# Banded attention and two FFN layers: four output buffers per tile instead of two

## The chip, the cores and the metric

The kernel runs on one core of one Trainium2 chip. The metric is device time in microseconds, from the start to the end of one execution. The core has five engines that run side by side, each with a queue of its own that it works off in order: TensorE (PE, with its weight loads listed apart as PEld), VectorE (DVE), ScalarE (ACT), GpSimd (POOL) and SyncE (SP), which here only issues DMAs. TensorE writes its results to PSUM, eight banks of 128 x 512 floats; VectorE and ScalarE copy them from there to SBUF, and a DMA takes them from SBUF to device memory.

## What is computed

Attention over a band with sinks, for 4 batches, 8 heads, 768 positions and 64 dimensions a head, and behind it two feed-forward layers over 3072 tokens (512 wide, 2048 hidden), all in float32:

```python
keep = is_sink | in_window                      # first 4 keys, and the last 128
scores = np.where(keep, scale * q @ k.T, -1e9)
a = np.exp(scores - scores.max(-1, keepdims=True))
a = a / (a.sum(-1, keepdims=True) + 1e-9)
x = a @ v                                       # -> 3072 tokens x 512
h = x @ w1_in;  x = (h - np.tanh(h)) @ w1_out   # layer 1
h = np.maximum(x @ w2_in, 0.0)
out = (h * h) @ w2_out                          # layer 2
```

## The kernel before

Float32 products are made from two parts of each operand, a high one and the rest (`split`, lines 147 to 151), with three matmuls for each product: high by high, high by low, low by high. Weights, activations and attention probabilities all go through this.

**Layer 1** (`ffn`, lines 434 to 524) takes the tokens in 8 tiles of 384. A tile walks over 16 chunks of the hidden dimension. `mm1` (12 matmuls, line 451) makes a chunk's hidden values in a PSUM bank, `ps_h`, of which there is one; `act` (lines 455 to 468) forms `h - tanh(h)` in a tile `t` (two buffers) and splits it into `gs`; `mm2` (12 matmuls, lines 483 and 485) adds the chunk's part to the tile's four results, `acc`, one PSUM bank each, four banks in all. A chunk's `mm2` is issued one chunk late, two chunks late in the last tile (`lag`). The tile's last `mm2` therefore runs while the next tile's first chunk is in work, and it ends with the four evictions, lines 487 to 498. Between the matmuls of tile j a hook (`hook`, lines 826 to 843) sets the attention of tile j + 1, head by head, and the conversion of layer 2's weights, piece by piece.

**Layer 2** (`Second`, lines 557 to 788) takes the tokens in 6 tiles of 512, and a tile in 8 groups of 256 hidden units. It makes the first product by seven products of sums of blocks (`first`, `rest`) and the second one directly (`second`), one group late, again with four results in the four `acc` banks, evicted in lines 749 to 757. A tile's inputs come from device memory by four DMAs (`load_x`) into the tiles `xs`; GpSimd makes four sums of them, three in new tiles and one in place (`sum_x`), and ScalarE and GpSimd split seven operands out of them (`split_x`) into `xop`. `xs` has seven buffers, just what a tile's inputs and sums take. The second layer's output weights are fetched group by group into four buffers, named `wi`, `wo`, `wos2` and `wos3` (`fetch_out`, line 609).

**What sets the order.** TensorE's order is that of the source, written out by hand. The instructions of the other engines and of SyncE are put in order at compile time by a planner that steps through the program with estimated times: an instruction is placed once its inputs are there and a buffer for its output is free, and those with the lower number go first. The evictions have their number lowered by 200 (`high_priority`), the DMAs behind them don't. Tiles of one `tag` share its `bufs` buffers: one is handed on to a later tile when all readers of the old tile are done, and the instructions that fill it wait for those readers on the chip. So an eviction into `o` waits, with two buffers, for the store of the result two before it.

Result m of a tile goes to VectorE where m is odd and to ScalarE where it is even. In layer 1 each is copied to `o` (lines 488 to 494) and stored to `x2` in device memory (line 496, `x<-o` in the trace); in layer 2 it is copied to `o` (lines 750 to 756) and stored to the output (line 757, `out_dram<-o`). The branch `l == 1` of `ffn` belongs to `general`, the path for other sinks and windows, which these inputs don't take.

Of the kernel before, what the change touches and what calls it, by code (L numbers as in the profile page):

```python
# [11 lines left out]
F32 = mybir.dt.float32  # L12
# [7 lines left out]
P = 128  # L20
# [4 lines left out]
T = 384  # L25
# [12 lines left out]
HT = T2 // 2  # L38
NG = FC // 2
NP = 7  # L40
# [106 lines left out]
def split(c, dst, src, lo_eng):  # L147

    nc = c.nc
    nc.scalar.activation(dst[:, 0, :], src, AF.Copy)  # L150
    lo_eng.tensor_tensor(dst[:, 1, :], src, dst[:, 0, :].bitcast(F32), ALU.subtract)  # L151
# [282 lines left out]
def ffn(c, layers, xs, hook=None):  # L434


    nc = c.nc
    accs = {}

    def lag(l, j):  # L440
        return 2 if l == 1 or j == NT - 1 else 1

    def mm1(l, j, fc, x, q):
        w = layers[l].get(0, fc).rearrange("p a (k f) -> p a k f", f=P)
        if q == 0:
            tag = ("ps_h", "ps_s", "ps_t", "ps_v")[fc % 4] if l == 1 or j == NT - 1 else "ps_h"
            c.hb = c.ps.tile([P, 512], F32, tag=tag, name=tag, bufs=1)
        h = c.hb
        for kc in range(2 * q, 2 * q + 2):
            for i, (a, b) in enumerate(((0, 0), (0, 1), (1, 0))):  # L450
                nc.tensor.matmul(h[:, :T], w[:, a, kc, :], x[kc][:, b, :], start=(kc == 0 and i == 0),  # L451
                                 stop=(kc == KC - 1 and i == 2))
        return h

    def act(l, h, j, fc):
        t = c.fp.tile([P, T], F32, tag="t", name="t", bufs=2)
        if lag(l, j) > 1 and fc % 2:
            gs = c.spare(fc)[:, : 2 * T].rearrange("p (a t) -> p a t", t=T)
        else:
            gs = c.fp.tile([P, 2, T], F32R, tag="gs", name="gs", bufs=2)  # L460
        if l == 0:
            c.last_a = nc.scalar.activation(t, h[:, :T], AF.Tanh)  # L462
            c.last_d = nc.vector.tensor_tensor(t, h[:, :T], t, ALU.subtract)  # L463
        else:
            c.last_a = nc.scalar.activation(t, h[:, :T], AF.Relu)
            c.last_d = nc.vector.scalar_tensor_tensor(t, h[:, :T], 0.0, t, ALU.max, ALU.mult)
        split(c, gs, t, nc.vector if l > 0 or j > 0 else nc.gpsimd)
        return gs

    def mm2(l, j, fc, gs, q):  # L470
        w = layers[l].get(1, fc)
        if fc == 0 and q == 0:
            accs[l, j] = [c.ps.tile([P, 512], F32, tag="acc", name="acc", bufs=4) for _ in range(KC if l == 0 else T // P)]
        acc = accs[l, j]
        pas = ((0, 0), (0, 1), (1, 0))
        n = len(acc)
        work = [(m, i) for m in range(n) for i in range(3)]
        hw = (len(work) + 1) // 2
        for m, i in work[q * hw : (q + 1) * hw]:
            a, b = pas[i]  # L480
            st = dict(start=(fc == 0 and i == 0), stop=(fc == FC - 1 and i == 2))
            if l == 0:
                nc.tensor.matmul(acc[m][:, :T], w[:, a, ts(m, P)], gs[:, b, :], **st)  # L483
            else:
                nc.tensor.matmul(acc[m], gs[:, b, ts(m, P)], w[:, a, :], **st)
        if fc == FC - 1 and q == 1:
            for m in range(n):
                o = c.fp.tile([P, 512], F32, tag="o", name="o", bufs=2)
                wd = T if l == 0 else 512
                with c.tc.high_priority(offset=200):  # L490
                    if m % 2:
                        nc.vector.tensor_copy(o[:, :wd], acc[m][:, :wd])
                    else:
                        nc.scalar.activation(o[:, :wd], acc[m][:, :wd], AF.Copy)  # L494
                if l == 0:
                    nc.sync.dma_start(c.x2[m, :, ts(j, T)], o[:, :T])
                else:
                    nc.sync.dma_start(c.out[j * T + m * P : j * T + (m + 1) * P, :], o)

    pend = []  # L500
    for l in range(len(layers)):
        for j in range(NT):
            x = xs(l, j)
            for fc in range(FC):
                late = pend[: len(pend) - lag(l, j) + 1]
                pend = pend[len(late) :]
                if hook:
                    hook(l, j, fc, 0)
                mm1(l, j, fc, x, 0)
                if hook:  # L510
                    hook(l, j, fc, 1)
                h = mm1(l, j, fc, x, 1)
                gs = act(l, h, j, fc)
                if hook:
                    hook(l, j, fc, 2)
                for p in late:
                    mm2(*p, 0)
                    if p is late[-1] and hook:
                        hook(l, j, fc, 3)
                    mm2(*p, 1)  # L520
                if not late and hook:
                    hook(l, j, fc, 3)
                pend.append((l, j, fc, gs))
    return [lambda p=p, q=q: mm2(*p, q) for p in pend for q in range(2)]


# [30 lines left out]
class Second:  # L557
# [179 lines left out]
    def second(self, j, g, s, q):  # L737

        c, nc = self.c, self.c.nc
        if g == 0 and q == 0:  # L740
            self.acc = [c.ps.tile([P, 512], F32, tag="acc", name="acc", bufs=4) for _ in range(4)]
        seen = ((1, 1), (0, 0)), ((1, 0), (0, 1))
        for th, f in seen[q]:
            w, gs = self.wo[2 * g + f], s.g[th, f]
            for m in range(2):
                for i, (a, b) in enumerate(((0, 0), (0, 1), (1, 0))):
                    nc.tensor.matmul(self.acc[2 * th + m], gs[:, b, ts(m, P)], w[:, a, :],  # L747
                                     start=(g == 0 and q == 0 and i == 0), stop=(g == NG - 1 and q == 1 and i == 2))
                if g == NG - 1 and q == 1:
                    o = c.fp.tile([P, 512], F32, tag="o", name="o", bufs=2)  # L750
                    k = 2 * th + m
                    with c.tc.high_priority(offset=200):
                        if m:
                            nc.vector.tensor_copy(o, self.acc[k])  # L754
                        else:
                            nc.scalar.activation(o, self.acc[k], AF.Copy)
                    nc.sync.dma_start(c.out[j * T2 + k * P : j * T2 + (k + 1) * P, :], o)
# [222 lines left out]
```

## Time and profile before

| | |
|---|---|
| median of 3 runs | 1304.63 us (1301.48 to 1305.8) |
| the profiled execution | 1303.22 us |
| its span, first to last instruction | 1301.3 us |
| TensorE busy | 1245.7 us, 96% |
| VectorE busy | 816.4 us, 63% |
| ScalarE busy | 644.6 us, 50% |
| GpSimd busy | 396.5 us, 30% |
| DMA | 158.27 MB, mean 122 GB/s |
[...]

The span has four parts: about 54 us with the loads and the attention of the first tile, layer 1 with the attention of the tiles to come until about 790 us, layer 2 until 1294 us, and the last stores. The rows below are given by engine and line. "x6" is a count of instructions, the number in front of the engine is the start in microseconds and the one behind it the time, and square brackets hold the time for which the engine stood idle before the row and what released it. `x<-o` is the DMA from the tile `o` to the buffer `x2`; the program's names stand without numbers.

### The profile page before, as it was taken

What the parts mean: (1) busy time and instruction counts of PE and PEld (TensorE: products, weight loads), DVE (VectorE), ACT (ScalarE), POOL (GpSimd) and SP (SyncE); (2) the same over time, 40 slices, a digit from 0 to 9 for tenths busy, and PEclk for the clock granted to TensorE, in tenths of its full rate; (3) what the DMA queues carried; (4) which work ended last, traced back from release to release, by engine and by line L of the source; (5) the groups of instructions that cost most, each with busy time, mean ns of one, the idle gap of its engine ahead of it and who ended that gap; (6) DMA issues with size and microseconds to landing.
All of it is one profiled execution on the core that took longest, in us unless ns stands there. A gap on an engine that the chain in (4) does not pass through costs nothing.

```text
span 1301.3 us, 21253 instructions
## 1 busy us (share of the span) xinstructions
PE 1245.7 (96%) x7632; PEld 1167.3 (90%) x7632; DVE 816.4 (63%) x2004; ACT 644.6 (50%) x1690; POOL 396.5 (30%) x381
## 2 busy tenths in 40 slices
PE   7888899999899999999999999999999999999997
PEld 5777799999799999999999998999989999999996
DVE  7888667777776677676675675454464544644543
ACT  7766566666566667666665552232232322323221
POOL 1555632323233334343332402050140410503100
PEclk9999899999999999999999999999999999999999
DMA  9641134443333333333322233343352433533432
GB/s 365 245 173 49 54 116 128 127 146 117 95 117 107 119 103 102 114 101 114 116 69 90 89 91 128 105 139 134 109 162 100 130 130 98 162 97 99 140 105 82
DMA packets 67795, 158.27 MB, mean 122 GB/s; under 512 B 6864, under 2 KB 29392, under 8 KB 67680
## 3 DMA queue, kind: packets, MB, share of 16 engines
q1 hardware_dynamic: 67680, 156.82, 37.1%
q8 instruction: 62, 1.02, 0.3%
q14 instruction: 53, 0.43, 0.1%
HBM read 131.63 MB, written 25.17 MB: 120 GB/s over the span
## 4 chain that ended last, share of the span: by engine, by line
PE 72%; DVE 10%; DMA 8%; ACT 4%; issue 2%; POOL 1%; SPq 0%; ACTq 0%; DVEq 0%; POOLq 0%
PE acc L747 20%; PE acc L483 14%; PE ps_h L451 12%; PE ps_h L696 5%; PE ps_v L696 5%; PE ps_t L696 5%; DMA wos<-in_w_in_dram 5%; DVE w_bit L135 3%; PE ps_s L696 3%; DMA x<-o 2%; DVE w_bit L134 2%; PE ps_t L318 2%; DVE w_bit L133 2%; PE ps_s L269 1%; PE ps_v L359 1%
## 5 line engine op out<-in xcount | busy, mean ns | idle before, releaser
L483 PE MATMUL acc<-gs,wo 128*128 128x384 f32 x1440 | 300.4, 346 | 10.3 <-ACT o L494 10.3
L451 PE MATMUL ps_h<-x,wi 128*128 128x384 f32 x1392 | 293.1, 346 | 1.0 <-DVE t L463 1.0
L483 PEld LDWEIGHTS acc<-gs,wo 128*128 128x128 f32 x1440 | 247.9, 190 | 14.3 <-ACT o L494 11.8
L451 PEld LDWEIGHTS ps_h<-x,wi 128*128 128x128 f32 x1392 | 238.1, 189 | 3.8 <-DVE t L463 3.0
L150 ACT ACTIVATE x<-gs 128x256 fp32r<-128x256 f32 x144 | 54.8, 412 | 203.9 <-DVE gs L713 130.1
L151 POOL TENSOR_TENSOR x<-gs,x 128x256 fp32r<-128x256 f32 x48 | 35.6, 741 | 351.0 <-ACT x L150 351.0
L747 PE MATMUL acc<-wos,x 128*128 128x512 f32 x576 | 139.5, 391 | 0.0
L747 PEld LDWEIGHTS acc<-wos,x 128*128 128x128 f32 x576 | 105.2, 188 | 19.9
L463 DVE TENSOR_TENSOR t<-ps_h,t 128x384 f32<-128x384 f32 x116 | 64.7, 557 | 86.9 <-ACT t L462 86.9
L218 POOL TENSOR_TENSOR k_l<-qkv,k_h 128x416 fp32r<-128x416 f32 (+1 forms) x48 | 60.6, 1262 | 113.7 <-ACT k_h L217 113.1
L278 ACT ACTIVATE p<-p,nm 128x272 f32<-128x272 f32 (+1 forms) x168 | 83.5, 497 | 20.7 <-DVE nm L271 19.4
L271 DVE CUSTOM_DVE_ANT_0 p<-ps_s,m 128x272 f32<-128x272 f32 (+1 forms) x168 | 69.6, 414 | 31.7 <-PE ps_s L270 29.9
L288 DVE TENSOR_SCALAR p<-p,sm 128x272 f32<-128x272 f32 (+1 forms) x168 | 78.8, 492 | 2.2
L151 POOL TENSOR_TENSOR wos<-w_bit,wos 128x256 fp32r<-128x256 f32 x32 | 23.6, 738 | 184.7 <-ACT wos L150 103.3
L150 ACT ACTIVATE gs<-t 128x384 fp32r<-128x384 f32 x120 | 62.7, 523 | 30.1 <-DVE t L463 27.8
L747 PE MATMUL acc<-wo,x 128*128 128x512 f32 x288 | 74.8, 395 | 2.5 <-DMA wo<-wo 2.5
L747 PE MATMUL acc<-wi,x 128*128 128x512 f32 x288 | 74.9, 394 | 0.4 <-DVE o L754 0.4
L151 DVE TENSOR_TENSOR gs<-t,gs 128x384 fp32r<-128x384 f32 x104 | 60.7, 584 | 12.4 <-ACT gs L150 12.0
L151 POOL TENSOR_TENSOR xop<-xs,xop 128x512 fp32r<-128x512 f32 x42 | 57.2, 1388 | 35.7 <-ACT xop L150 35.7
L303 ACT ACTIVATE pt<-ps_t 128x384 fp32r<-128x384 f32 (+1 forms) x112 | 51.6, 461 | 29.2 <-PE ps_t L318 28.4
L747 PEld LDWEIGHTS acc<-wo,x 128*128 128x128 f32 x288 | 53.1, 190 | 12.7 <-issue 2.7
L747 PEld LDWEIGHTS acc<-wi,x 128*128 128x128 f32 x288 | 53.0, 190 | 11.2 <-DVE o L754 1.1
(186 smaller groups left out, 2526.7 us busy)
## 6 DMA issues: line engine op xcount, KB each, us to landing
wos<-wo SPq DMA_DIRECT2D x48, 512.0 KB, 4.1
qkv<-in_a_dram SPq DMA_DIRECT2D x32, 608.0 KB, 4.3
wi<-wo SPq DMA_DIRECT2D x24, 512.0 KB, 3.2
wo<-wo SPq DMA_DIRECT2D x24, 512.0 KB, 4.2
qkv<-in_a_dram SPq DMA_DIRECT2D x24, 504.0 KB, 3.8
wi<-in_w_in_dram SPq DMA_DIRECT2D x16, 512.0 KB, 9.6
wo<-in_w_out_dram SPq DMA_DIRECT2D x16, 512.0 KB, 9.2
wos<-in_w_in_dram SPq DMA_DIRECT2D x32, 256.0 KB, 2.9
```

The costliest lines, as they stand in the source:

```text
L150: nc.scalar.activation(dst[:, 0, :], src, AF.Copy)
L151: lo_eng.tensor_tensor(dst[:, 1, :], src, dst[:, 0, :].bitcast(F32), ALU.subtract)
L218: nc.gpsimd.tensor_tensor(s.kl[:, :nk], s.k[:, :nk], s.kh[:, :nk].bitcast(F32), ALU.subtract)
L271: nc.vector.tensor_tensor_reduce(out=s.p[:, u, :w], in0=sc[:, :w], in1=self.masks[kind], op0=ALU.add, op1=ALU.min, scale=-SCALE / 2 if ful ...
L278: self.mark[n] = nc.scalar.activation(s.p[:, u, :w], s.p[:, u, :w], AF.Exp, bias=s.nm[:, u : u + 1], scale=-1.0, accum_out=s.sm[:, u : u + 1])
L288: nc.vector.tensor_scalar(s.p[:, u, :w], s.p[:, u, :w], s.sm[:, u : u + 1], None, ALU.mult)
L303: nc.scalar.activation(hi, src, AF.Copy)
L451: nc.tensor.matmul(h[:, :T], w[:, a, kc, :], x[kc][:, b, :], start=(kc == 0 and i == 0), stop=(kc == KC - 1 and i == 2))
L463: c.last_d = nc.vector.tensor_tensor(t, h[:, :T], t, ALU.subtract)
L483: nc.tensor.matmul(acc[m][:, :T], w[:, a, ts(m, P)], gs[:, b, :], **st)
L696: self.c.nc.tensor.matmul(bank, w[:, a, kc, :], x[:, b, kc, :], start=start and kc == 0 and i == 0, stop=kc == 1 and i == 2, skip_group_ch ...
L747: nc.tensor.matmul(self.acc[2 * th + m], gs[:, b, ts(m, P)], w[:, a, :], start=(g == 0 and q == 0 and i == 0), stop=(g == NG - 1 and q == ...
```

## The change

The tile's four results no longer go through two buffers. In layer 1, results 0 to 2 get three buffers `o` of 384 columns, and result 3 one of the two buffers of the tag `t`, which `act` uses for the chunk's hidden values. In layer 2 the results share the seven buffers `xs` with the next tiles' inputs and sums. In the path not taken they share `x`. The copies, the stores, their engines and their priority are the same.

```diff
             for m in range(n):
-                o = c.fp.tile([P, 512], F32, tag="o", name="o", bufs=2)
                 wd = T if l == 0 else 512
+                if l == 1:
+                    o = c.xp.tile([P, 512], F32, tag="x", name="x", bufs=8)
+                elif m < 3:
+                    o = c.fp.tile([P, T], F32, tag="o", name="o", bufs=3)
+                else:
+                    o = c.fp.tile([P, T], F32, tag="t", name="t", bufs=2)
                 with c.tc.high_priority(offset=200):
...
                 if g == NG - 1 and q == 1:
-                    o = c.fp.tile([P, 512], F32, tag="o", name="o", bufs=2)
+                    o = c.l2.tile([P, 2, HT], F32, tag="xs", name="xs", bufs=NP).rearrange("p a t -> p (a t)")
                     k = 2 * th + m
                     with c.tc.high_priority(offset=200):
```

## Rows read from the trace of the kernel before

**Rows 1.** Windows: stretch, its length, busy time by engine, granted clock, DMA share, GB/s.
```profile
168.00:785.00 617.00, 597.28 (x3729) 586.66 (x3728) 436.52 (x1154) 395.85 (x1054) 203.47 (x208) 1.00 0.35 110
...
860.00:1290.00 430.00, 429.63 (x2687) 388.58 (x2687) 217.20 (x458) 115.97 (x286) 97.99 (x91) 1.00 0.38 121
```
**Rows 2.** Waits of TensorE's matmuls, whole span: us in total, times, longest.
```profile
PE acc L483 <- ACT o L494: 10.3, 6, 2.9
...
PE acc L747 <- DMA wo<-wo: 2.5, 1, 2.5
```
**Rows 3.** Tile `o`: idle time before its writers (us, times), and its stores.
```profile
  DMA x<-o: 30.7, 13
...
DMA to landing us min/median/max: 1.9/2.9/6.2
```
**Rows 4.** Timeline of the boundary between tiles 3 and 4 of layer 1.
```profile
448.00 0.68 DVE L151 TENSOR_TENSOR gs<-t,gs 128x384 fp32r<-128x384 f32 x1
...
450.65 1.05 PEld L483 LDWEIGHTS acc<-gs,wo 128*128 128x128 f32 x6
...
451.02 0.49 ACT L462 ACTIVATE t<-ps_h 128x384 f32<-128x384 f32 x1
...
454.93 0.49 ACT L494 ACTIVATE o<-acc 128x384 f32<-128x384 f32 x1 [3.42 <-DMA x<-o]
...
455.48 1.20 PEld L483 LDWEIGHTS acc<-gs,wo 128*128 128x128 f32 x6 [3.12 <-ACT o L494]
```
**Rows 5.** Waits of TensorE's weight loads, whole span.
```profile
PEld acc L483 <- ACT o L494: 11.8, 6, 3.2
PEld ps_s L269 <- DVE nm L271: 11.1, 12, 2.3
...
PEld acc L747 <- DVE o L754: 1.1, 2, 0.8
```
**Rows 6.** Timeline of the boundary between tiles 4 and 5 of layer 1.
```profile
546.78 0.20 PEld L318 LDWEIGHTS ps_t<-ident,p 128*128 128x128 f32 x2 [1.73 <-DVE pt L305]
```
**Rows 7.** Windows after the standstill of rows 4, and around the one at 634.
```profile
457.60:458.60 1.00, 1.00 (x5) 1.00 (x5) 0.76 (x2) 0.11 (x1) 0.00 (x0) 0.50 0.00 0
...
634.00:636.00 2.00, 1.56 (x10) 1.46 (x11) 1.59 (x5) 2.00 (x6) 0.00 (x0) 1.00 0.36 125
```
**Rows 8.** Timelines of weight loads behind two boundaries, the same sequence in both.
```profile
267.20 1.00 PEld L483 LDWEIGHTS acc<-gs,wo 128*128 128x128 f32 x6 [1.08 <-ACT o L494]
...
270.27 1.00 PEld L451 LDWEIGHTS ps_h<-x,wi 128*128 128x128 f32 x6
...
460.14 1.00 PEld L451 LDWEIGHTS ps_h<-x,wi 128*128 128x128 f32 x6
```
**Rows 9.** Timelines in layer 2: loads of inputs, last split, first eviction.
```profile
943.41 4.29 SPq L672 DMA_DIRECT2D xs<-x  x4
...
952.37 1.47 POOL L151 TENSOR_TENSOR xop<-xs,xop 128x512 fp32r<-128x512 f32 x1
...
959.32 0.60 ACT L756 ACTIVATE o<-acc 128x512 f32<-128x512 f32 x1 [0.82 <-PE acc L747]
```
**Rows 10.** Timeline of the end: the last matmuls and the last copy.
```profile
1287.93 5.60 PE L747 MATMUL acc<-wos,x 128*128 128x512 f32 x24
...
1295.44 0.69 DVE L754 COPY o<-acc 128x512 f32<-128x512 f32 x1 [2.54 <-DMA out_dram<-o]
```
**Rows 11.** Timeline of SyncE between the layers.
```profile
787.51 2.14 SPq L496 DMA_DIRECT2D x<-o  x2
789.74 0.38 SPq L609 DMA_DIRECT2D wo<-wo  x1
...
792.52 0.32 SPq L496 DMA_DIRECT2D x<-o  x1
```
**Rows 12.** Timeline of ScalarE between tiles 6 and 7 of layer 1.
```profile
722.88 0.63 ACT L150 ACTIVATE xop<-xs 128x512 fp32r<-128x512 f32 x1 [0.59 <-POOL xs L681]
```
**Rows 13.** Waits of TensorE's weight loads from 275 to 355 us.
```profile
PEld ps_s L269 <- DVE nm L271: 7.6, 7, 2.2
```

## The prediction

> **What bounds the kernel now.** I began with the busy time by stretch, to see which engine has no room. In layer 1 beyond its first tile (168 to 785 us) TensorE is busy 597.28 of 617 us and VectorE 436.52, ScalarE 395.85; in layer 2 from its second tile on it is 429.63 of 430 [rows 1]. So an edit can win only where TensorE stands still: layer 2's steady part has 0.4 us to give, layer 1 some 20 us, and the two ends of the span what they show.
>
> Second, the waits of TensorE by releaser. The largest in layer 1 is the one the change aims at: the first matmuls of a tile into `acc` waited six times for ScalarE's eviction L494, 10.3 us in all [rows 2]. Third, the view of the tile `o`: before the evictions ScalarE and VectorE sat idle 30.7 us in 13 cases until a store `x<-o` had landed, and a store lands 1.9 to 6.2 us after its issue, 2.9 in the median [rows 3]. Those 30.7 us are not the price: TensorE had other matmuls during most of them. The price is TensorE's own standstill.
>
> Fourth, the timeline of one boundary, to see the mechanism. In [rows 4] result 2 is ready before TensorE begins the next tile at 450.65, but ScalarE evicts it at 454.93, after 3.42 us of idling until a store had landed; the stores of results 0 and 1 hold the two buffers. TensorE's weight loads stop for 3.12 us, until 455.48. ScalarE is blocked whole for that time, as its queue runs in order.
>
> **The change part by part.** *Layer 1, the wait.* Four buffers (three `o`, one `t`) remove the wait of evictions 2 and 3 for stores 0 and 1. I take the price from the weight loads, because they follow each other without a gap here while matmul spans overlap: 11.8 us in six waits [rows 5], and a seventh, 1.73 us, where VectorE was held by its own `o` and so released a transposition late [rows 6]: 13.5 us. By the matmul rows the six cost 10.3 [rows 2]; that is the lower end. [...]
>
> What is late next at a boundary? The two freed evictions, about 0.5 us on ScalarE and 0.56 on VectorE, now stand earlier, ahead of the hidden chunk's splits. In [rows 4] the low half of `gs` starts at 448.00, ends at 448.68, and is wanted at 450.65: 2 us of cover against 0.56. ScalarE's tanh of the next chunk was done at 451.02 + 0.49, before the standstill, so nothing else of that chunk was late. I cost this move at nothing; if its cover were gone it would be 0.56 us at each of seven boundaries, 3.9.
>
> *Layer 1, the clock.* [...] From the restart to the second block of `ps_h` weights the slow case took 460.14 - 455.48 = 4.66 us [rows 4, 8], the same sequence at full clock 270.27 - 267.20 = 3.07 [rows 8]. With the standstill goes that 1.6. [...]
>
> *Layer 1, the buffer in `t`.* Result 3 takes one of the two `t` buffers for a copy and a store. If buffers are handed on in the order of the source, the next chunk's tanh takes the other one, whose last reader is that same low half, done at 448.68, while the tanh runs at 451.02 [rows 4]. No wait. That it goes otherwise is a rival.
>
> *Layer 2, the boundaries.* Evictions 3 and 4 no longer wait for stores: 1.1 us of weight loads in two waits [rows 5]; the matmuls were idle 0.37 us there [rows 1]. I take 1.1.
>
> *Layer 2, the shared buffers.* The four results share `xs`, seven buffers, with the next tile's inputs and sums. Three added waits: evictions on what was in the buffer, inputs and sums on the stores. The first: VectorE and ScalarE reach the evictions at 959.32; GpSimd's last split of the old contents ended at 952.37 + 1.47 = 953.8 [rows 9]. Cover 5.5 us. The second: loads `xs<-x` were issued at 943.41, before these evictions [rows 9], and if buffers are handed on in the order of the source they must now follow them, some 20 us later, with the four sums on GpSimd; they are needed only at the end of the next tile, and a tile lasts (1293.5 - 789.7) / 6 = 84 us [rows 10, 11]. SyncE's fetches of `wos` may stand behind a load that waits for a store, by up to one landing, 2.9 us; TensorE, busy 429.63 of 430 us, waited for none of them [rows 1]. All cost nothing in this trace; if the last cover failed, five boundaries times 2.9 are 14 us.
>
> *The end.* The last matmul of 24 ends at 1287.93 + 5.60 = 1293.53. Without waits the last copy starts near 1293.6 instead of 1295.44 [rows 10]: 1.9 us. The four stores of 256 KB then lie closer, so I take 1.7, bounds 1.4 and 1.9.
>
> *Between the layers.* The first matmuls of layer 2 waited 2.5 us for a weight fetch [rows 2] issued at 789.74, behind the stores of results 0 and 1 [rows 11]. With no wait in ScalarE, store 2 can come ahead of it: one more issue, 0.3 us. Bounds: 1.8 us gained, if it goes right behind store 0 at 787.9, or 3.1 lost, if store 3 comes ahead too and that is issued only at 792.52 as now, the fetch at 792.9 [rows 11].
>
> Sum: 13.5 + 1.6 + 1.1 + 1.7 - 0.3 = 17.6 us. The profiled execution took 1303.2 us (span 1301.3, 1.9 around it): 1285.6. The median of the runs shown is 1.4 us higher, so I forecast 1287 on its footing.
>
> **The rivals.** *The queue keeps the stall.* The buffer is free, but evictions stay behind other work in an in-order queue. For it: between tiles 6 and 7 ScalarE evicts result 2 only behind a split, at 722.88, that had waited for GpSimd [rows 12], and TensorE lost the longest wait there, 3.2 [rows 5]. Against it: at [rows 4] nothing but the store was waited for. If half of the 13.5 stays, 6.8: 1294.
>
> *The `t` buffer stalls the tanh.* If the next tanh gets result 3's buffer, it waits for that store. With the copy done near 448.7 and a landing of 2.9 it runs at 451.6 instead of 451.02, hidden; at the longest landing, 6.2, at 454.9, and the one `ps_h` bank is then released about 2 us after TensorE wants it. Seven times 2 us is 14: about 1301, no change. Against it: the other buffer is free 2.3 us before.
>
> *The queues are planned anew, slower.* The orders of the other engines come from a planner that knows when a buffer is free; after the first boundary they will differ. In one tile of the trace, 275 to 355 us, TensorE waited seven times for VectorE's score reduction, 7.6 us of the 11.1 that the whole span has of this wait [rows 5, 13]. If the new order makes that pattern the rule, each further tile costs 7.6; 17.6 / 7.6 = 2.3, so from three tiles on the kernel is slower: 1310 with three, 1317 with four. Against it: all other tiles together have 3.5 us of it.
>
> *Better than forecast.* The same lottery takes those 7.6 us away too: 1279.
>
> **How the numbers follow.** Forecast 0.62, kept stall 0.20, better 0.06, `t` stall 0.06, slower order 0.06. Two executions of this kernel can be told apart from about 0.3%, 3.9 us. Faster by more: 0.62 + 0.20 + 0.06 = 0.88; within: 0.06; slower: 0.06. The forecast with its bounds (3 less for matmul rows, 1.6 for the clock, 3.1 at the layers' border, 3 of luck either way) holds 1282 to 1292; with the kept stall and part of the better case the range is 1281 to 1297.
>
> **What would show it.** Right: no idle time of ScalarE or VectorE for `x<-o` or `out_dram<-o`; no wait of `acc` for L494 in layer 1; evictions 0 to 3 within 2 us at each boundary; the last copy within 1 us of the last matmul; the span some 17 us shorter, 15 of them before 785 us. Wrong: standstills at the same places with another releaser, tanh waiting for a store, more `ps_s` waits for VectorE, the fetch between the layers later than 790 us, or layer 2 longer than its 84 us a tile.

## The result, and the profile after

The changed kernel takes 1290.95 us in the median (1289.55 to 1291.18) against 1303.97 us (1301.48 to 1305.8) for the kernel before: 13.0 us less, a ratio of 0.9896 with a 95% interval of 0.9872 to 0.9921. The profiled execution's span went from 1301.3 to 1289.4 us, 11.9 less. The forecast was 17.6 us less, 1287 us. The direction and the range are right. By the medians 4.6 us of the forecast gain are missing, by the profiled spans 5.7, and the experiments look for them.

The evictions themselves went as forecast. In the view of the tile `o` (lines of the changed kernel: 499 is ScalarE's eviction, 497 VectorE's, 501 the store) the 30.7 us of idling for stores [rows 3] are gone, though a store now lands later, 4.2 us after its issue in the median against 2.9:

```profile
L499 ACT ACTIVATE o<-acc x16: 472/486/493, 171.1 to 781.1; 128x384 f32<-128x384 f32 x16
L497 DVE COPY o<-acc x8: 543/546/550, 172.0 to 780.6; 128x384 f32<-128x384 f32 x8
its engine sat idle before it (us, times) until:
  PE acc L483: 0.7, 1
...
DMA to landing us min/median/max: 1.9/4.2/6.4
```

The boundary between tiles 3 and 4, whose old form is in [rows 4], in the timeline of the changed kernel:

```profile
448.50 1.00 PEld L483 LDWEIGHTS acc<-gs,wo 128*128 128x128 f32 x6
...
449.66 1.05 PEld L483 LDWEIGHTS acc<-gs,wo 128*128 128x128 f32 x6
449.67 0.47 ACT L499 ACTIVATE o<-acc 128x384 f32<-128x384 f32 x1
...
450.26 0.55 DVE L497 COPY o<-acc 128x384 f32<-128x384 f32 x1
...
451.10 0.49 ACT L499 ACTIVATE o<-acc 128x384 f32<-128x384 f32 x1
451.40 1.41 SPq L501 DMA_DIRECT2D x<-o  x3
451.61 0.55 DVE L497 COPY t<-acc 128x384 f32<-128x384 f32 x1
```

Four evictions start within 2 us, result 3 goes to `t`, and the weight loads follow each other: the standstill of 3.12 us is gone, and so is the half clock behind it [rows 7].

The end, and layer 2's loads of inputs, answer to [rows 9] and [rows 10]. The last copy starts 0.04 us after the last matmul; the loads `xs<-x` now follow the evictions and come 20 us later against the weight loads around them (953.39, against 943.41 less the 10.0 us by which the kernel is ahead there):

```profile
949.49 0.60 ACT L761 ACTIVATE xs<-acc 128x512 f32<-128x512 f32 x1 [0.90 <-PE acc L752]
...
953.39 2.61 SPq L677 DMA_DIRECT2D xs<-x  x4
...
1277.40 5.60 PE L752 MATMUL acc<-wos,x 128*128 128x512 f32 x24
...
1283.04 0.69 DVE L759 COPY xs<-acc 128x512 f32<-128x512 f32 x1 [0.67 <-PE acc L752]
```

What is missing lies in layer 1. Busy time by stretch (length, then PE, PEld, DVE, ACT, POOL, granted clock, DMA share, GB/s), first the kernel before, with layer 1 cut in two:

```profile
168.00:440.00 272.00, 261.83 (x1626) 252.70 (x1625) 199.34 (x550) 178.02 (x491) 90.42 (x92) 1.00 0.39 120
440.00:785.00 345.00, 335.45 (x2105) 333.95 (x2104) 237.19 (x605) 217.83 (x564) 113.04 (x117) 1.00 0.32 102
```

and the changed kernel:

```profile
168.00:440.00 272.00, 259.16 (x1611) 250.15 (x1610) 198.39 (x544) 176.93 (x488) 89.63 (x91) 1.00 0.37 118
440.00:785.00 345.00, 342.78 (x2168) 341.31 (x2166) 246.09 (x624) 222.56 (x574) 120.82 (x122) 1.00 0.34 107
```

From 440 us on TensorE has 7.3 us more work in the same time. Before 440 us it has 2.7 us less: in this execution that stretch got worse. To find where, I put the n-th weight load of one trace beside the n-th of the other; TensorE's order is the source's, so they are the same work. The start in the changed kernel minus that in the other, at times of the kernel before (us; the rows below the first belong to the experiments, and the two pairs at the end are at the times of e3 and of e6, with the last product in the column 1290; e3 reaches the boundary between tiles 3 and 4 at 440, and the value there is the one ahead of it):

```
                          168    275    440    640    740    800   1290
changed - before        +0.30  +4.05  +2.74  -6.32  -7.81  -9.70 -10.75
e1  - before            +0.03  +4.31  +0.03  -9.02 -10.87 -10.79 -11.58
e2  - before            -0.81  -1.25  -2.35  -4.31  -4.57  -4.21  -5.04
e7  - before            +1.09  +5.44  +1.13  -7.89  -9.31  -9.25 -10.30
e9  - before            -0.01  +2.31  +0.63  -2.18  -3.51  -4.80  -5.86
e4  - e3                +0.03  -2.71  -4.44 -11.03 -11.89 -13.62 -14.17
e5  - e6                +0.88  -2.21  -3.50 -14.87 -16.19 -17.88 -18.00
```

Step by step, the seven boundaries of layer 1 gain 1.5, 1.1, 0.6, 4.7, 1.8, 2.5 and 3.2 us: 15.4, and the forecast had 13.5 + 1.6 = 15.1. But more than the first is given back within 20 us, in two steps of 1.6 and 1.7, and more than the second within 10 us, most of it in one step of 2.6; of the seventh 1.7 are given back. Net of small steps, tile 1 gives back 3.6 us, tile 2 2.5 and the last tile 1.7, and tile 3 regains 0.4: some 7.3 together. Net, layer 1 gains 8.1.

Two rows of the table show how much of this belongs to one execution. The instructions of layer 1 up to its last tile stand in the same order in e1, e7 and the changed kernel, and in e2 and the kernel before. From 168 to 440 us the changed kernel lost 2.4 us, e1 and e7 nothing, and e2 gained 1.5. So the loss by 275 us is there each time (4.3 us in e1 and in e7, 3.8 in the changed kernel, boundaries included), while the net of the first half is uncertain by some 2 us.

Two timelines show the first give-back. Behind the boundary between tiles 0 and 1, the changed kernel:

```profile
173.43 0.54 DVE L497 COPY t<-acc 128x384 f32<-128x384 f32 x1
...
175.72 0.46 SPq L579 DMA_DIRECT2D wos<-in_w_in_dram  x1
...
179.62 0.43 ACT L132 ACTIVATE wos<-wos 128x256 f32<-128x256 f32 x1 [1.75 <-DMA wos<-in_w_in_dram]
...
180.40 0.26 ACT L303 ACTIVATE pts<-ps_t 64x128 fp32r<-64x128 f32 x1
...
180.57 1.21 POOL L218 TENSOR_TENSOR k_l<-qkv,k_h 128x416 fp32r<-128x416 f32 x1 [8.62 <-ACT k_h L217]
180.88 1.18 DVE L135 SCALAR_TENSOR_TENSOR w_bit<-wos,w_bit 128x256 int32<-128x256 int32 x1
...
182.45 0.28 DVE L305 TENSOR_TENSOR pts<-ps_t,pts 64x128 fp32r<-64x128 f32 x1
...
182.79 0.19 PEld L373 LDWEIGHTS ps_v<-pts,v_k 128*128 128x128 f32 x1 [1.49 <-DVE pts L305]
```

and the kernel before, the same work:

```profile
174.95 0.43 SPq L574 DMA_DIRECT2D wos<-in_w_in_dram  x1
...
179.46 0.42 ACT L132 ACTIVATE wos<-wos 128x256 f32<-128x256 f32 x1
...
180.55 0.25 ACT L303 ACTIVATE pts<-ps_t 64x128 fp32r<-64x128 f32 x1
180.70 0.42 DVE L135 SCALAR_TENSOR_TENSOR w_bit<-wos,w_bit 128x256 int32<-128x256 int32 x1
...
180.72 1.34 POOL L218 TENSOR_TENSOR k_l<-qkv,k_h 128x416 fp32r<-128x416 f32 x1 [9.08 <-ACT k_h L217]
...
182.41 0.19 PEld L373 LDWEIGHTS ps_v<-pts,v_k 128*128 128x128 f32 x1
```

In tiles 1 and 2 the hook converts `w2_in`, layer 2's input weights: a load into the one buffer `wos`, ScalarE's L132 on it, VectorE's L133 to L135, a store, the next load. The load does not get the time that TensorE gained at the boundary: it is issued 0.77 us later than before (175.72 and 174.95), of which 0.3 were there at 168 us and the rest is VectorE's copy of result 3, which now stands ahead of L133. L132 runs at nearly the same time in both kernels (179.62 and 179.46). Before, ScalarE came to L132 when the load had landed, as the standstill at the evictions had held back the rest. Now it comes 1.75 us early, waits, and the attention's `pts` copy stands behind it in the queue. `L135`, which took 0.42 us when it began just ahead of GpSimd's L218 and takes 1.18 behind its start, adds the rest, and TensorE waits 1.49 us. L135 ends 0.28 us after L218 here (182.06 and 181.78), and again behind the next boundary (275.60 and 275.32). What makes it longer beside L218 no run shows.

The largest step, 2.6 us behind the boundary between tiles 1 and 2, has the same parts in other sizes. The view of the load's line in a window with this one load, first of the kernel before (issued at 265.73), then of the changed kernel (issued at 268.11), and the changed kernel's timeline:

```profile
DMA to landing us min/median/max: 3.2/3.2/3.2
```

```profile
DMA to landing us min/median/max: 4.7/4.7/4.7
```

```profile
272.86 0.44 ACT L132 ACTIVATE wos<-wos 128x256 f32<-128x256 f32 x1 [2.47 <-DMA wos<-in_w_in_dram]
...
274.12 1.48 DVE L135 SCALAR_TENSOR_TENSOR w_bit<-wos,w_bit 128x256 int32<-128x256 int32 x1
```

The load lands 1.5 us later after its issue, and L135 takes 1.1 us more than its 0.42: together the 2.6. All four stores of the tile were issued just ahead of this load, where before two came ahead of it and two behind. So here the load did not keep its pace, it became slower. That the bunched stores did it is likely but not shown: the load issued at 182.52, with no store of results still under way, landed 4.2 us after its issue against 2.8 before.

### The profile page after: what moved, and what is told of

The parts are those of the page before. It is cut to its first block, busy times and chain, and to the rows that moved or that the text cites. A ratio compares the mean times of both kernels' runs of the same rounds, so it can differ in the third digit from the quotient of the medians.

```text
span 1289.4 us, 21277 instructions
## 1 busy us (share of the span) xinstructions
PE 1241.6 (96%) x7632; PEld 1164.7 (90%) x7632; DVE 817.9 (63%) x2004; ACT 646.4 (50%) x1690; POOL 398.1 (31%) x381
## 4 chain that ended last, share of the span: by engine, by line
PE 76%; DVE 10%; DMA 5%; ACT 3%; issue 2%; SPq 0%; POOL 0%; ACTq 0%; DVEq 0%; POOLq 0%
PE acc L752 20%; PE acc L483 15%; PE ps_h L451 13%; PE ps_h L701 5%; PE ps_v L701 5%; PE ps_t L701 5%; DMA wos<-in_w_in_dram 4%; DVE w_bit L135 3%; PE ps_s L701 3%; DVE w_bit L134 2%; PE ps_t L318 2%; DVE w_bit L133 1%; PE ps_s L269 1%; PE ps_s L270 1%; PE ps_v L359 1%
## 5 line engine op out<-in xcount | busy, mean ns | idle before, releaser
L150 ACT ACTIVATE x<-gs 128x256 fp32r<-128x256 f32 x144 | 55.0, 412 | 200.4 <-DVE gs L718 125.8
L151 POOL TENSOR_TENSOR x<-gs,x 128x256 fp32r<-128x256 f32 x48 | 35.9, 748 | 332.6 <-ACT x L150 332.6
L218 POOL TENSOR_TENSOR k_l<-qkv,k_h 128x416 fp32r<-128x416 f32 (+1 forms) x48 | 60.5, 1260 | 114.6 <-ACT k_h L217 114.0
L150 ACT ACTIVATE gs<-t 128x384 fp32r<-128x384 f32 x120 | 62.7, 523 | 32.3 <-DVE t L463 30.0
L151 POOL TENSOR_TENSOR wos<-w_bit,wos 128x256 fp32r<-128x256 f32 x32 | 23.6, 739 | 174.7 <-ACT wos L150 72.0
L151 POOL TENSOR_TENSOR xop<-xs,xop 128x512 fp32r<-128x512 f32 x42 | 58.1, 1414 | 35.7 <-ACT xop L150 35.7
L151 DVE TENSOR_TENSOR gs<-t,gs 128x384 fp32r<-128x384 f32 x104 | 60.7, 584 | 12.9 <-ACT gs L150 12.6
```

The lines of the kernel that those rows point to most:

```text
L218: nc.gpsimd.tensor_tensor(s.kl[:, :nk], s.k[:, :nk], s.kh[:, :nk].bitcast(F32), ALU.subtract)
```

## The experiments

**My theory (A):** tiles 1 and 2 are paced by the conversion's round trip through one buffer, so what the boundaries gain there is given back. Rivals: the moved evictions or the buffer in `t` cost something themselves; the planner's new order is just worse; the boundaries had less to give.

**One part at a time.** e1 has the change in layer 1 only (layer 2's results go in turn through two other buffers, one of their own and `wos`), e2 in layer 2 only.

```diff
 # e1, on the changed kernel, layer 2's eviction
-                    o = c.l2.tile([P, 2, HT], F32, tag="xs", name="xs", bufs=NP).rearrange("p a t -> p (a t)")
+                    if m == 0:
+                        o = c.l2.tile([P, 512], F32, tag="o2", name="o", bufs=1)
+                    else:
+                        o = c.fp.tile([P, 512], F32, tag="wos", name="o", bufs=1)
 # e2, on the kernel before
-                    o = c.fp.tile([P, 512], F32, tag="o", name="o", bufs=2)
+                    o = c.l2.tile([P, 2, HT], F32, tag="xs", name="xs", bufs=NP).rearrange("p a t -> p (a t)")
```

> The change in layer 1 alone; layer 2's four results go through two buffers as before. From the weight loads of the two traces, taken one by one, layer 1 with the border to layer 2 gave 9.7 us, layer 2's boundaries 1.05 and the end 1.4. If the two parts are independent: 1304 - 9.7 = 1294.3, that is 2.5 us over the changed kernel. Rival, the gain of layer 1 hangs on the plan of the whole program: a time more than 2 us from 1294.

> The change in layer 2 alone. If the parts are independent: 2.5 us less than before, 1301.5, with the standstills of acc for L494 in layer 1 all back (10.3 us by matmuls) and the last copy right behind the last matmul. Rival, the shared xs buffers cost something that layer 1's gain covers in the changed kernel: not below before, 1304 or more.

Measured beside a kernel before of 1302.74: e1 1292.91 (0.992, 0.9891 to 0.9949), 9.8 us less; e2 1300.85 (0.9972, 0.9951 to 0.9994), 1.9 less. Together 11.7 of the 13.0, so the parts are independent within the spread of the runs, and layer 1 carries most of it. By 275 us e1 is 4.3 us behind the kernel before, the whole change 4.1 (table above): the loss there is layer 1's own.

**The conversion's loads taken out, with the old and with the new buffers.** Without the loads L132 never waits for a landing.

```diff
 # e3 on the kernel before, e4 on the changed kernel, in the conversion's step
-                if step + 1 < 2 * FC:
-                    self.load(c.w2_in, step + 1)
```

> The kernel before, without 31 of the 32 loads of layer 2's input weights in tiles 1 and 2 of layer 1: all conversions work on the first piece, so the output is not the reference's. Theory A, tiles 1 and 2 are paced by a round trip of one buffer (load, ScalarE, VectorE, store, next load), about 5.3 us a chunk: without the loads tile 1 falls from 90.9 us towards the 86 of tiles 3 and 5, tile 2 from 99 towards the 93 of tile 4, 4 to 10 us in all, 1294 to 1300. Theory B, it is VectorE's and ScalarE's work in those tiles and the order of their queues, not the loads: within 2 us of before.

> The changed kernel with the same loads left out. Theory A: the 3.3 and 3 us that boundaries 0/1 and 1/2 gave back are the loads' round trip, so here they are kept and the distance to the kernel before without loads is 17 us or more, not 13; the time is 1277 to 1283. Theory B: the distance stays at 13 or less, as the evictions, pulled ahead on VectorE, still make its score reductions late.

e3 took 1292.23 us (0.9923, 0.9896 to 0.995), e4 1274.05 (0.9786, 0.9759 to 0.9812). The change is now worth 18.2 us by the medians, 15.4 by the two profiled spans (1285.7 and 1270.3), and the table's row for the pair has no give-back in tiles 1 and 2: -2.71 at 275, -4.44 at 440, where the changed kernel had +4.05 and +2.74. That is what theory A asks for, though both kernels came out faster than the ranges expected of them. The kernel before loses 10.5 us to the loads as well, so the pace was there before the change. Taking the loads out also takes out their traffic; the next pair keeps it.

**All the work done, but the loads in two buffers in turn.** The loads of `w2_in` alternate between `wos` and `w_bit`, so that one is under way while the other is converted: e5 with the new output buffers, e6 with the old ones.

```diff
 # in load
-        t = c.fp.tile([P, 2, DM // 2], I32, tag="wos", name="wos", bufs=1).rearrange("p a c -> p (a c)")
+        if src is c.w2_in and i % 2:
+            t = c.sb.tile([P, DM], I32, tag="w_bit", name="w_bit", bufs=3)
+        else:
+            t = c.fp.tile([P, 2, DM // 2], I32, tag="wos", name="wos", bufs=1).rearrange("p a c -> p (a c)")
 # in the conversion's step: the next load is issued first
-                self.convert_in(step)
+                now = self.early
                 if step + 1 < 2 * FC:
                     self.load(c.w2_in, step + 1)
+                nxt, self.early = self.early, now
+                self.convert_in(step)
+                self.early = nxt
```

> The changed kernel; the loads of layer 2's input weights alternate between the buffer wos and one of the three buffers w_bit, and each is issued ahead of the conversion before it. All work is there. Theory A (the round trip through one buffer paces tiles 1 and 2): close to the kernel without these loads, 1274 to 1281, ScalarE's wait for wos loads (30.8 us in 31 cases) below 5 us. If what the missing loads gave was the DMA traffic itself, or the time on SyncE, it stays at 1288 to 1291.

> The kernel before with the same alternating loads. Theory A: as without the loads, 1290 to 1297, and the distance to the changed kernel with them, 15 to 18 us, is larger than the 13 of the change alone. Otherwise 1300 or more.

e5 took 1276.7 us (0.9799, 0.9778 to 0.982), e6 1294.79 (0.9936, 0.9916 to 0.9955). Here the change is worth 18.1 us, and e5 beats both kernels: 14.3 us below the changed one by the medians, 12.6 by the two ratios. The traffic is all there, so it is the single buffer that paced these tiles. By the times alone the step from 13 to 18 us is about as large as its uncertainty, as each ratio is known to some 3 us; the rows of the table and the waits below carry it: from 168 to 440 us the change gains 4.4 us in this pair and 4.5 in the other, where the changed kernel lost 2.4 and e1 and e7 nothing. In the first half of layer 1 TensorE is now never short of work for long; window of e5:

```profile
168.00:440.00 272.00, 271.71 (x1729) 269.14 (x1729) 207.05 (x581) 184.98 (x520) 94.00 (x97) 1.00 0.40 127
```

Waits of its weight loads from 168 to 440 us (us, times, longest), the changed kernel and then e5:

```profile
PEld ps_s L269 <- DVE nm L271: 10.6, 14, 1.8
PEld ps_v L373 <- DVE pts L305: 4.0, 2, 2.6
```

```profile
PEld ps_s L269 <- DVE nm L271: 1.6, 5, 0.6
```

So the score reduction, of which [rows 5] and [rows 13] show the waits, was for the most part late because it stood behind the conversion. ScalarE's waits over the span, the kernel before and the changed one, say the same from the other side; in e5 there is no such line:

```profile
ACT wos L132 <- DMA wos<-in_w_in_dram: 26.4, 30, 2.3
```

```profile
ACT wos L132 <- DMA wos<-in_w_in_dram: 30.8, 31, 2.5
```

**Without the buffer in `t`.** e9 gives layer 1 three buffers `o` and no share of `t`.

```diff
 # e9, on the changed kernel, layer 1's eviction
-                elif m < 3:
-                    o = c.fp.tile([P, T], F32, tag="o", name="o", bufs=3)
                 else:
-                    o = c.fp.tile([P, T], F32, tag="t", name="t", bufs=2)
+                    o = c.fp.tile([P, T], F32, tag="o", name="o", bufs=3)
```

> The changed kernel with three buffers o for the four results of layer 1 and none in t. Result 3 waits again for the store of result 0, VectorE with it. If sharing t costs anything in the changed kernel, this is as fast or faster: 1288 to 1291. If not, VectorE's wait at seven boundaries costs part of the old standstill: result 2, which released TensorE, goes free, so 2 to 6 us of the 15 come back, 1293 to 1297.

1297.5 us (0.9962, 0.9947 to 0.9978): 6.5 us above the changed kernel by the medians, 5.2 by the profiled spans (1294.6 and 1289.4), 0.5 us above the range expected if sharing `t` costs nothing. Some half of the gain is the fourth buffer, and taking it from `t` costs nothing that would outweigh this. A fourth buffer outside `t` was not run, so a small price of the sharing is not excluded. The waits of weight loads in layer 1 from 168 to 785 us, and the idle time before the evictions, both of e9, where result 3 now waits for the store of result 0:

```profile
PEld acc L483 <- DVE o L495: 7.6, 6, 2.7
...
  DMA x<-o: 16.3, 7
```

**The last boundary of layer 1.** ScalarE's five splits L150 of layer 2's first inputs stand ahead of a tanh there. Timeline of the changed kernel:

```profile
716.52 2.72 ACT L150 ACTIVATE xop<-xs 128x512 fp32r<-128x512 f32 x5 [0.62 <-POOL xs L686]
719.14 0.47 ACT L462 ACTIVATE t<-ps_t 128x384 f32<-128x384 f32 x1
719.64 0.56 DVE L463 TENSOR_TENSOR t<-ps_t,t 128x384 f32<-128x384 f32 x1 [7.26 <-ACT t L462]
...
731.30 0.19 PEld L483 LDWEIGHTS acc<-gs,wo 128*128 128x128 f32 x1 [0.95 <-ACT gs L150]
...
731.90 1.17 PEld L483 LDWEIGHTS acc<-gs,wo 128*128 128x128 f32 x7 [0.41 <-DVE gs L151]
```

A first try, e7, moved the seven splits three chunks down in the source.

```diff
 # e7, in the tile's hook, instead of at its head
+                if fc == 3 and q == 0:
+                    for name in ORDER:
+                        second.split_x(0, name)
```

> The changed kernel; the seven splits of layer 2's first inputs stand in the source three chunks later, so that ScalarE does not hold chunk 2's tanh of tile 7 behind splits that wait for GpSimd's sums. In the changed kernel that tanh stood 5.4 us after its bank was ready and TensorE lost 1.8 us between 725 and 732. If that is the cause: 1.5 to 2 us less than the changed kernel, 1289. If the 1.8 us come from VectorE's side (its subtractions for layer 2's weights beside GpSimd): no change, 1291.

1291.04 us (0.9906, 0.9887 to 0.9926), no change; but the planner put the splits almost where they had been, with the tanh at 716.73 still behind them, and the 1.8 us stayed. It says nothing about the cause. e10 forces the places: one split a chunk, each behind that chunk's last tanh on ScalarE; e11 is the same on e5.

```diff
 # e10 on the changed kernel, e11 on e5, in the last tile's hook
-        for name in ORDER:
-            self.split_x(0, name)
...
+                if q == 3 and 2 <= fc < 2 + NP:
+                    with tc.issue_after(c.last_a.ins):
+                        second.split_x(0, ORDER[fc - 2])
```

> The changed kernel, with the seven splits of layer 2's first inputs spread: one in each chunk of layer 1's last tile from the third chunk on, each behind that chunk's last tanh on ScalarE, instead of all at the head of the tile. Theory A (what the changed kernel gives back between tiles 6 and 7, about 1.8 us of weight loads, is ScalarE standing behind those splits, with the tanh of a chunk queued behind them): the standstills of the weight loads for the low half of gs between 724 and 733 us go, and the time is 1289, 1.5 to 2 below the 1291 of the changed kernel. Theory B (it is VectorE, slowed beside GpSimd's sums, that is late there): the standstills stay, 1291. In both, tiles 1 and 2 of layer 1 are as they were.

> The same spreading of the seven splits on top of the kernel whose loads of layer 2's input weights alternate between two buffers (1276.7 by the median). If the two causes are independent, as theory A has it: 1275, 1.5 to 2 less. If the last boundary's loss is VectorE's (theory B): 1277, no change. Against the kernel before: 0.979 or 0.980.

e10 took 1288.95 us (0.9883, 0.9866 to 0.99) and e11 1275.8 (0.9779, 0.9765 to 0.9794). By the times alone neither is told from its parent (1290.95, 1276.7). The trace of e10 decides: from 726 to 732 us it gains 1.7 us of weight loads on the changed kernel, the waits for `gs` are gone, and the tanh stand ahead of the splits, though VectorE's L642 (L644 in the changed kernel) still takes 1.49 us beside GpSimd's L151, against 0.43 at 720.50, with GpSimd done at 720.18:

```profile
717.21 0.49 ACT L462 ACTIVATE t<-ps_v 128x384 f32<-128x384 f32 x1 [2.52 <-PE ps_v L451]
717.60 0.63 ACT L150 ACTIVATE xop<-xs 128x512 fp32r<-128x512 f32 x1
...
718.97 1.49 DVE L642 TENSOR_TENSOR xs<-x 128x256 f32<-128x256 f32 x1 [0.68 <-POOL xop L151]
```

So the 1.8 us are ScalarE's queue (theory A), not VectorE. In the profiled executions of e10 and e11 the gain is lost again at the border of the layers, 2.2 and 1.6 us: in e10 1.6 with a clock that fell to 0.50 (below) and 0.6 with a longer wait, 2.98 us against 2.37; in e11, whose wait there is e5's, 2.8 us, the mean granted clock of the span is 0.991 against e5's 0.993.

## Why the prediction was right in sign and range, and 4 us off

**The sum, term by term** (by weight loads, forecast and measured):

| term | forecast | measured |
|---|---|---|
| layer 1, seven boundaries and the clock | 15.1 | 15.4 |
| given back behind them in layer 1, net | 0 | -7.3 |
| between the layers | -0.3 | 1.9 |
| layer 2, boundaries | 1.1 | 1.05 |
| the end | 1.7 | 1.2 |
| ahead of 168 us | 0 | -0.3 |
| sum | 17.6 | 11.9 |

**The step that failed** is "What is late next at a boundary? ... I cost this move at nothing". I looked for what is late within one boundary, in [rows 4], and that boundary lies in a tile where nothing else paces the work; there the step held, and 4.7 us were gained where 3.12 + 1.6 had been forecast. The next late thing in tiles 1 and 2 is no split of `gs` but the load of `w2_in`, which I did not price, and behind the first boundary the moved eviction of result 3 made this load 0.5 us later still; 7.3 us were given back in layer 1 where the sum has 0. Of tiles 1 and 2 the prediction names only [rows 13] and takes its 7.6 us for an accident of the planner's order, a rival either way. It was a symptom. After the change the same stretch, 275 to 355 us, has 5.5 us of it, and with the loads in two buffers the whole span has 4.0. Where the conversion is out of the way, the change is worth 18.2 (e3 to e4) or 18.1 us (e6 to e5) by the medians, close to the sum of 17.6. The profiled spans of the two pairs give 15.4 and 19.0. They differ by 3.6, of which the clock is, by my estimate, 3.2, two falls of 1.6: in e6 it was at 0.50 behind two standstills of layer 1 (from 536 to 538 us and from 624.5 to 627.5), and its mean over the span is 0.988 against 0.994 in e3.

**The price of the waits** was right: 15.4 against 15.1 by weight loads. The matmul rows would have made it smaller, 10.3 us for the six waits against 11.8 [rows 2, 5]; that the whole sum would be 3 us smaller by them, as the range has it, no run shows.

**The clock** came back with its 1.6 at the boundary of [rows 4]. That the range goes 1.6 lower for it was my estimate, as no row shows when the clock falls; the runs showed that the fall is not there each time. In e2, whose layer 1 is that of the kernel before, the weight loads stood 2.83 us at the same boundary, until 452.84, and the clock stayed at 1.00:

```profile
453.00:455.00 2.00, 2.00 (x14) 1.90 (x15) 1.97 (x7) 1.40 (x5) 0.00 (x0) 1.00 0.55 197
```

**Between the layers** I took 0.3 us lost and had 1.8 gained as a bound. The fetch did go out right behind store 0; SyncE in the changed kernel, against [rows 11]:

```profile
781.17 0.33 SPq L501 DMA_DIRECT2D x<-o  x1
781.59 0.38 SPq L614 DMA_DIRECT2D wo<-wo  x1
```

But the weight loads still stood 2.37 us there, 2.66 before, and TensorE waited for this fetch 2.2 us by matmul rows against 2.5 [rows 2]. The 1.9 is 0.3 of that and 1.6 of the clock, which had fallen to half behind this standstill in the execution before (0.50 from 795 to 797 us) and did not after (1.00 from 786 to 788): a term that I had not looked for at this place, and one that is there again in e10 (0.50 from 786 to 788). This is luck: without it the profiled execution would have gained 10.3 us and not 11.9.

**Layer 2 and the end** were right to 0.5 us. The sharing of `xs` cost nothing: the loads came 20 us later, as forecast, and the tiles did not grow. From the last matmul's end to the end of the span it went from 7.8 to 6.4 us, 1.4 against 1.7 (1.2 by the weight loads of the table).

**The range** held in part by luck as well. It allowed for a smaller gain by the matmul rows, the clock, the fetch between the layers and a kept stall; what came short was none of these.

**The rivals.** *The queue keeps the stall* (1294) comes closest in time, but not in mechanism: no weight load of `acc` waits for an eviction any more. What was kept is a different in-order queue: ScalarE's, with the conversion's load in it in tiles 1 and 2 and the splits of layer 2's inputs between tiles 6 and 7, and the place of [rows 12] did show the second. *The `t` buffer* is out: no tanh waited for a store, and e9 is slower without it. *The queues planned anew* gave no new order that makes the pattern of [rows 13] the rule.

## What to carry to other kernels

A standstill at one place also lets everything else catch up, so its length is the gain only where nothing else paces the work: for each stretch look for a loop with one buffer (here load, convert, store, next load) whose step is nearly as long as the work beside it, and do not count the gain there until that loop has a second buffer. One typical boundary is not enough; look at each stretch in which the beside-work differs. Here the output buffers brought 13 us alone, the second load buffer 7 (e6), and both together 25 (e5).

## What the runs showed of the chip

The half clock behind a standstill of TensorE does not go by the standstill's length alone. It fell to 0.50 behind 3.12 us [rows 7], 2.66 us (kernel before, border of the layers) and 2.98 us (e10, border), and stayed at 1.00 behind 3.21 us (kernel before, 723.94). Windows of the kernel before, behind 3.21 and behind 2.66 us:

```profile
723.00:725.00 2.00, 1.06 (x6) 1.06 (x7) 0.00 (x0) 2.00 (x5) 2.00 (x2) 1.00 0.12 45
...
795.00:797.00 2.00, 2.00 (x6) 1.60 (x5) 0.00 (x0) 0.00 (x0) 0.06 (x1) 0.50 0.29 105
```

and of e10 behind the 2.98 us:

```profile
786.00:788.00 2.00, 2.00 (x6) 1.54 (x6) 0.00 (x0) 0.00 (x0) 0.00 (x0) 0.50 0.00 0
```

What decides it no run here shows. It cost 1.6 us behind the 3.12 [rows 4, 8], and as much behind the 2.66 and the 2.98: from the first weight loads of `acc` to those of `ps_t` it is 5.04 us in the kernel before (793.84 to 798.88) and in e10 (784.00 to 789.04), 3.45 in the changed kernel (785.73 to 789.18). The run-to-run spread goes with the granted clock: of 18 runs of the kernel before on one chip the two slowest, 1309.95 and 1309.05 us, had a mean granted clock of 0.986, the two fastest, 1298.83 and 1298.96, of 0.992 and 0.994. Whether the changed kernel varies less is open: its 4 runs lie within 1.6 us, but those of e10, which has even fewer waits, within 5.2.
